# Loads of values and memory values get an earlier due time in the planner of a fused attention and MLP kernel

## The chip, the cores and the metric

The kernel runs on one core of a Trainium2 chip. The metric is the device time of one execution in microseconds, the median of several runs. Five engines run their own instruction streams in order: TensorE (PE, with its weight loads as PEld), VectorE (DVE), ScalarE (ACT), GpSimd (POOL) and SyncE (SP). SP computes nothing: it issues DMAs, one after the other, and an issue that waits for a semaphore holds back all that stand behind it.

## What is computed

```python
for c in range(nc):                       # 24 chunks of 32 rows, 4 batches, 8 heads of 64
    l_start = max(0, c * 32 - 16); r_end = min(S, c * 32 + 32 + 8)
    k_full = np.concatenate([mem_k, k[:, :, l_start:r_end]], axis=2)
    v_full = np.concatenate([mem_v, v[:, :, l_start:r_end]], axis=2)
    a = softmax(scale * q_c @ k_full^T)
    out[:, :, c_start:c_end] = a @ v_full
x = out.transpose(0, 2, 1, 3).reshape(3072, 512)
x = (sigmoid(x @ w_gate) * (x @ w_val)) @ w_out        # inner width 1536
h = x @ w_in                                           # inner width 2048
return (h * sigmoid(1.702 * h)) @ w_out2
```

All inputs are float32. Local attention with 8 memory rows gives 3072 rows of 512; two gated MLPs follow.

## The kernel before, in words

**Products.** The MLPs run as products of 128x128 weights and 512 columns, each operand split into a high and a low part, three products for one. `first_product` (L821, L828) multiplies the attention's rows with w_gate and w_val, the gating stands at L845 to L856, `gemm2` (L1020) multiplies with w_out. The second MLP is built from combined blocks (L1318, L1655) and takes the time from about 470 us on.

**Attention.** It is cut into 32 tiles of 96 rows (three chunks, 8 heads). Six prologue tiles run ahead of the first MLP product, with q and k transposed on TensorE (L436, L444) and with buffers of their own. The tiles after that run inside the first MLP. The last 23 of them are late tiles: their q and k are loaded in 32-row pieces (12 loads for q, 16 to 20 loads for the k of two tiles), transposed on DVE (L532 q, L540 k), the scores are computed on TensorE (L555), softmax runs on DVE and ACT (L572 to L615), POOL normalises (L623), DVE transposes the weights into `pt` (L670), and TensorE multiplies `pt` with the values (L704, "PV"). On TensorE the PV of one late tile and the scores of the next form one burst.

**Values.** `load_ctx` (L407) loads the values of a tile and its 8 memory values into `vn` (names `in_v_dram` and `in_mem_v_dram` in the profile): two loads, three for a tile at the edge of a batch, together 256 KB. All tiles but the prologue's share one buffer `vn`, so a tile's loads wait for the PV of the tile before. In the trace the buffers of q, k and the normalised weights bear the names of memory that they share: `f` is q of a late tile, `raw` is k or the normalised weights.

**What sets the order.** All instructions are tasks of one list scheduler (`Schedule`, L73 to L130). Going backwards, a task's due time is the smallest of its successors' due times less the latency between, less its own duration and less its `slack`. Going forwards, each engine takes of the tasks that are ready by the planner's clock the one with the lowest due time. A task's due time passes on to all that it depends on, so a lower due time of a load also lowers those of the PV whose buffer it takes over, and of what that PV needs. Bursts have due times on a fixed pace (L605). In the prologue the planner fills gaps that it expects on TensorE with dummy products (L885).

**Issue.** Only SP issues the loads of q, k and v. POOL issues its own DMAs: loads of weights of the second MLP (`p_raw`, L292, 512 KB) and stores of prepared weights (`wo_dram`, L1429 256 KB and L1432 512 KB).

Of the kernel before, what the change touches and what calls it, by code (L numbers as in the profile page):

```python
# [33 lines left out]
class Schedule:  # L34
# [9 lines left out]
    def add(self, eng, dur, fn, r=(), w=(), nbytes=0, due=None, slack=0.0, margin=0.0, hold=0.0):  # L44
        i = len(self.tasks)
        deps = set()
        for x in r:
            if x in self.writer:
                deps.add(self.writer[x])
        for x in w:  # L50
            if x in self.writer:
                deps.add(self.writer[x])
            deps.update(self.readers.get(x, ()))
        for x in r:
            self.readers.setdefault(x, set()).add(i)
        for x in w:
            self.writer[x] = i
            self.readers[x] = set()
        deps.discard(i)
        self.tasks.append(  # L60
            dict(eng=eng, dur=dur, fn=fn, deps=deps, nbytes=nbytes, due=due, slack=slack, margin=margin, hold=hold, succ=[])
        )
        return i
# [82 lines left out]
def kernel(  # L146
# [39 lines left out]
    add = sch.add  # L186
# [155 lines left out]
        add(*(("dve", 0.7) if low_dve else ("pool", c_pool(512))), low, r=[kf, ("w", slot, 0)], w=[("w", slot, 1)])  # L342


    def dma(dst, src, key, r=(), act=False, dur=0.45, pool=False):
        n = 8
        for d in src.shape:
            n *= d
        q_ = nc.gpsimd if pool else nc.scalar if act else nc.sync
        add("pool" if pool else "act" if act else "sp", dur, lambda: q_.dma_start(out=dst(), in_=src), r=list(r), w=[key], nbytes=n)  # L350

    class Bufs:

# [36 lines left out]
    def attention(t, bufs, banks, pe_path, extra=None, nth=0, last=False):  # L390
# [9 lines left out]
        T = bufs.t  # L400
# [4 lines left out]
        def load_ctx(name, src, mem, act=False):  # L405

            s0 = j * TQ - LEFT  # L407
            r0 = LEFT if j == 0 else 0
            r1 = TK - RIGHT if j == TPB - 1 else TK
            parts = [(r0, r1, src[b, :, s0 + r0 : s0 + r1, :]), (TK, P, mem[b])]  # L410
            if j == 0:
                parts.append((0, LEFT, src[b, :, 0:LEFT, :]))
            if j == TPB - 1:
                parts.append((r1, TK, src[b, :, S - RIGHT : S, :]))
            ks = []
            for i, (a, z, s) in enumerate(parts):
                ks.append((kk[name], i))
                dma(lambda a=a, z=z: T[name][a:z], s.rearrange("h s d -> s h d"), ks[-1], r=pre, act=act)
            for i in range(len(parts), 4):
                ks.append((kk[name], i))  # L420
            return ks

        pre = [bufs.gate] if bufs.gate else []
# [4 lines left out]
        if pe_path:  # L428
            ident = bufs.ident
            dma(lambda: T["qn"], q[b, :, j * TQ : (j + 1) * TQ, :].rearrange("h s d -> s h d"), kk["qn"], r=pre)  # L430
            kkn = load_ctx("kn", k, mem_k)
            load_ctx("vn", v, mem_v)

            def pe_q():
# [32 lines left out]
        else:  # L467
            koff, n, fresh = extra
            if n:
# [5 lines left out]
                for hp in range(2):  # L475
                    for x in range(2):
                        r = hp * D + x * CH
                        d = slice(x * CH, (x + 1) * CH)
                        for p in range(NP):
                            dma(  # L480
                                lambda r=r, p=p: T["kb"][r : r + CH, p, lo:hi, :],
                                k[b, 2 * p + hp, s0 + lo * CH : s0 + hi * CH, d].rearrange("(c r) d -> r c d", r=CH),
                                (kk["kb"], r, p),
                                r=pre,
                                dur=0.62,
                            )
                        kh = k[b].rearrange("(p two) s d -> two s p d", two=2)[hp]
                        if lo:
                            dma(
                                lambda r=r: T["kb"][r + LEFT : r + CH, :, 0, :],  # L490
                                kh[0 : CH - LEFT, :, d],
                                (kk["kb"], r, "edge"),
                                r=pre,
                            )
                        if hi < nb:
                            dma(
                                lambda r=r: T["kb"][r : r + CH - LEFT, :, nb - 1, :],
                                kh[S - CH + LEFT : S, :, d],
                                (kk["kb"], r, "edge"),
                                r=pre,  # L500
                            )
            kkb = [(kk["kb"], r, p) for r in range(0, P, CH) for p in (0, 1, 2, 3, "edge")]
            if fresh:
                for hp in range(2):
                    for x in range(2):
                        r = hp * D + x * CH
# [6 lines left out]
                    r=[(kk["mn"], r) for r in range(0, P, CH)],  # L513
                    w=[kk["mt"]],
                )
            kqb = []
            for hp in range(2):
                for x in range(2):
                    r = hp * D + x * CH
                    qh = q[b].rearrange("(p two) s d -> two s p d", two=2)[hp]  # L520
                    for c in range(NCK):
# [6 lines left out]
                            r=pre,  # L528
# [131 lines left out]
        else:  # L660
# [14 lines left out]
            def rest():  # L675
                load_ctx("vn", v, mem_v)
                tadd(
                    "pool",
                    0.95,
                    lambda: norm(nc.gpsimd, T["pn"][:, :, 0:CTX], (0, TQ), (0, CTX)),  # L680
                    r=ke + [kk["sm"]],
                    w=[(kk["pn"], 0)],
                )
                tadd("pool", 0.6, ev_norm, r=ke + [kk["sm"]], w=[(kk["pn"], 1)])
                for part in range(4):
                    tadd(
                        "dve",
                        0.88,
                        lambda part=part: ev_pt(part),
                        r=[(kk["pn"], 0), (kk["pn"], 1)],  # L690
                        w=[(kk["pt"], part)],
                    )
# [371 lines left out]
    for b in range(NB - 2):  # L1064
        n = BLK
# [834 lines left out]
```

## Time and profile before

| | |
|---|---|
| time, median of 3 runs | 1135.66 us (1134.58 to 1137.0) |
| the profiled execution's own time | 1138.62 us |
| its span, first to last instruction | 1136.8 us |
| mean granted TensorE clock | 0.995 |
| PE busy | 1122.9 us (99%) |
| DVE busy | 843.9 us (74%) |
| ACT busy | 588.6 us (52%) |
| POOL busy | 158.9 us (14%) |

The profile is of one execution; all durations are from it. Busy is the time in which an engine executes; issuing a DMA and waiting are not in it. The granted clock is the share of full speed that the chip allows TensorE in a stretch: 1.00 is 2.4 GHz and 0.50 is 1.2 GHz. A releaser is what an idle engine waited for last, inferred from semaphores; where the named one was long done, it was another of those waited for.

### The profile page before, as it was taken

The numbers are of one execution on the slowest core, as the hardware profiler recorded it, in microseconds if no ns is written. First come the engines' busy times: TensorE is split into PE (matmuls) and PEld (weight loads), VectorE is DVE, ScalarE is ACT, GpSimd is POOL, SyncE is SP. The second block draws the span as 40 slices with busy tenths as digits, with TensorE's granted clock in tenths as the row PEclk, the third lists the DMA queues.
The fourth block names the chain that finished last, engine by engine and source line by source line (L and its number), as shares of the span: only waits on it lengthen the run. The fifth ranks groups of instructions, "written<-read, shape, count | busy, mean of one in ns | idle before, by whom it ended". The sixth has DMA issues, their size and how long they took to land.

```text
span 1136.8 us, 19523 instructions
## 1 busy us (share of the span) xinstructions
PE 1122.9 (99%) x7190; PEld 939.3 (83%) x7190; DVE 843.9 (74%) x1440; ACT 588.6 (52%) x972; POOL 158.9 (14%) x209
## 2 busy tenths in 40 slices
PE   9999999999999989999999999999999999999998
PEld 7888899988888867788888888888888888888886
DVE  7999757776677769798887787969966359575366
ACT  6887622223222344576766678657445365354452
POOL 5332244122433112200001110000000000000000
PEclk9999999999999989999999999999999999999999
DMA  9666244334433555553545867777797676786526
GB/s 208 217 206 203 75 127 102 54 63 120 95 88 75 149 126 158 191 177 120 177 166 188 321 232 270 254 291 268 240 263 217 199 202 213 239 220 198 174 82 178
DMA packets 245903, 203.13 MB, mean 179 GB/s; under 512 B 170928, under 2 KB 191920, under 8 KB 245808
## 3 DMA queue, kind: packets, MB, share of 16 engines
q1 hardware_dynamic: 225696, 168.33, 51.2%
q0 software_dynamic: 6880, 24.12, 5.7%
q10 hardware_dynamic: 13232, 9.44, 2.6%
q8 instruction: 57, 0.93, 0.3%
q14 instruction: 38, 0.31, 0.1%
HBM read 151.49 MB, written 50.33 MB: 178 GB/s over the span
## 4 chain that ended last, share of the span: by engine, by line
PE 95%; DMA 2%; DVE 1%; SPq 1%; ACT 0%; issue 0%; DVEq 0%; ACTq 0%
PE bank L1318 30%; PE bank L1655 20%; PE bank L1020 17%; PE bank L821 15%; PE bank L828 8%; PE both L704 2%; PE both L555 2%; DMA f<-in_q_dram 1%; SPq L350 1%; PE bank L885 1%; PE bank L704 0%; PE bank L645 0%; DVE pt L670 0%; DMA qn<-in_q_dram 0%; PE bank L444 0%
## 5 line engine op out<-in xcount | busy, mean ns | idle before, releaser
L1318 PE MATMUL bank<-sb_x,sb_r 128*128 128x512 f32 x1512 | 347.1, 389 | 0.0
L1318 PEld LDWEIGHTS bank<-sb_x,sb_r 128*128 128x128 f32 x1512 | 283.8, 188 | 58.9
L1655 PE MATMUL bank<-wq,w 128*128 128x512 f32 x756 | 178.0, 389 | 0.0
L1655 PEld LDWEIGHTS bank<-wq,w 128*128 128x128 f32 x756 | 141.8, 188 | 29.9 <-issue 0.4
L821 PE MATMUL bank<-xh,w 128*128 128x512 f32 (+1 forms) x464 | 160.5, 357 | 0.0
L821 PE MATMUL bank<-xl,w 128*128 128x512 f32 (+1 forms) x464 | 159.4, 355 | 0.0
L1334 DVE TENSOR_TENSOR sb_s<-bank,sb_s 128x512 f32<-128x512 f32 x108 | 74.4, 690 | 83.1 <-PE bank L1318 75.2
L828 PE MATMUL bank<-xh,w 128*128 128x512 f32 (+1 forms) x464 | 110.4, 360 | 0.0
L821 PEld LDWEIGHTS bank<-xh,w 128*128 128x128 f32 x464 | 88.6, 191 | 13.0
L1020 PE MATMUL bank<-gh,wq 128*128 128x512 f32 (+1 forms) x448 | 98.8, 361 | 0.0
L821 PEld LDWEIGHTS bank<-xl,w 128*128 128x128 f32 x464 | 88.4, 190 | 12.2
L1330 ACT ACTIVATE sb_s<-bank 128x512 f32<-128x512 f32 x108 | 64.7, 600 | 52.2 <-PE bank L1318 51.5
L828 PEld LDWEIGHTS bank<-xh,w 128*128 128x128 f32 x464 | 79.0, 191 | 12.6 <-issue 0.2
L1020 PEld LDWEIGHTS bank<-gh,wq 128*128 128x128 f32 x448 | 76.5, 189 | 13.1
L670 DVE STREAM_TRANSPOSE pt<-raw 32x256 f32<-32x256 f32 x184 | 79.6, 433 | 4.4 <-POOL raw L623 1.1
L1626 DVE TENSOR_TENSOR wq<-xh_g,wq 128x1024 fp32r<-128x1024 f32 (+1 forms) x60 | 60.5, 1008 | 24.3 <-ACT wq L1623 23.9
L1623 ACT ACTIVATE wq<-xh_g 128x1024 fp32r<-128x1024 f32 (+1 forms) x60 | 53.3, 888 | 34.5 <-PE bank L1655 33.6
L853 ACT ACTIVATE gh<-sig 128x512 fp32r<-128x512 f32 (+1 forms) x58 | 32.4, 559 | 74.8 <-DVE sig L848 71.7
L845 ACT ACTIVATE sig<-bank 128x512 f32<-128x512 f32 (+1 forms) x58 | 30.5, 526 | 64.1 <-PE bank L828 63.1
L1655 PE MATMUL bank<-wq,w_e 128*128 128x512 f32 x252 | 62.5, 389 | 0.0
L623 POOL TENSOR_TENSOR raw<-e,sm 96x448 f32<-96x448 f32 (+2 forms) x69 | 38.9, 574 | 166.0 <-DVE sm L615 125.6
L848 DVE SCALAR_TENSOR_TENSOR sig<-sig,bank 128x512 f32<-128x512 f32 (+1 forms) x58 | 34.0, 586 | 30.1 <-PE bank L828 29.4
(215 smaller groups left out, 1666.3 us busy)
## 6 DMA issues: line engine op xcount, KB each, us to landing
sb_r<-wc_dram SPq DMA_DIRECT2D x133, 256.0 KB
w<-wo_dram SPq DMA_DIRECT2D x63, 512.0 KB
w_e<-wo_dram SPq DMA_DIRECT2D x21, 512.0 KB
wc_dram<-sb_r SPq DMA_DIRECT2D x15, 512.0 KB
wo_dram<-w POOLq DMA_DIRECT2D x14, 512.0 KB, 3.7
raw<-in_moe_w_out_dram SPq DMA_DIRECT2D x13, 512.0 KB
raw<-in_moe_w_in_dram SPq DMA_DIRECT2D x13, 512.0 KB
wf_dram<-f POOLq DMA_DIRECT2D x24, 256.0 KB, 2.6
```

Source lines behind the costliest of these rows:

```text
L623: eng.tensor_tensor(out=dst, in0=e3()[r, :, c], in1=T["sm"][r].to_broadcast([n, H, keys[1] - keys[0]]), op=ALU.mult)
L670: nc.vector.transpose(T["pt"][r * CH : (r + 1) * CH, :, c * CH : (c + 1) * CH], T["pn"][c * CH : (c + 1) * CH, :, kb * CH : (kb + 1) * CH],)
L821: nc.tensor.matmul(bank[bk][:, :n], w[:, 0, ts[t]], x[xb][:, t, c0 : c0 + n], start=t == 0 and x is xhs, stop=False)
L828: nc.tensor.matmul(bank[bk][:, :n], w[:, 1, ts[t]], xhs[xb][:, t, c0 : c0 + n], start=False, stop=t == NK - 1)
L848: nc.vector.scalar_tensor_tensor(out=sig[:, :n], in0=sig[:, :n], scalar=1.0, in1=bank[src_val][:, :n], op0=ALU.add, op1=ALU.mult)
L1020: nc.tensor.matmul(bank[into[m]][:, c0 : c0 + n], w[:, wi, m * P : (m + 1) * P], g[:, :n], start=f == 0 and j == 0 and c0 == 0, stop=f == ...
L1318: nc.tensor.matmul(bank[bk], w[:, o : o + P], xt[x, k][:, xl, :], start=first and k == 0 and wl == 0 and xl == 0, stop=k == 1 and wl == 1, ...
L1330: add("act", c_act(BLK), lambda: nc.scalar.activation(work[n], bank[bk], AF.Copy), r=[("bank", bk)], w=[n])
L1334: nc.vector.tensor_tensor(out=work[n], in0=bank[bk], in1=work[n], op=ALU.add)
L1623: nc.scalar.activation(quad[b_][:, c, 0, :], src(js), AF.Copy)
L1626: nc.vector.tensor_tensor(out=quad[b_][:, c, 1, :], in0=src(js), in1=quad[b_][:, c, 0, :].bitcast(F32), op=ALU.subtract)
L1655: nc.tensor.matmul(bank[bk], lhs, quad[b_][:, x, gl_, :], start=begin, stop=last and x == js[-1] and wl == 1, skip_group_check=not first,)
```

## The change

`dma()` gets an argument `slack` that it hands to `add`, and `load_ctx` passes 5.0 us of it for `vn`, and 0.0 for `kn`. The due time of each load of values and memory values is 5 us earlier in the planner, for late tiles and for prologue tiles. No instruction is added or removed but for dummy products.

```diff
-    def dma(dst, src, key, r=(), act=False, dur=0.45, pool=False):
+    def dma(dst, src, key, r=(), act=False, dur=0.45, pool=False, slack=0.0):
...
-        add("pool" if pool else "act" if act else "sp", dur, lambda: q_.dma_start(out=dst(), in_=src), r=list(r), w=[key], nbytes=n)
+        add("pool" if pool else "act" if act else "sp", dur, lambda: q_.dma_start(out=dst(), in_=src), r=list(r), w=[key], nbytes=n, slack=slack)
...
-                dma(lambda a=a, z=z: T[name][a:z], s.rearrange("h s d -> s h d"), ks[-1], r=pre, act=act)
+                dma(lambda a=a, z=z: T[name][a:z], s.rearrange("h s d -> s h d"), ks[-1], r=pre, act=act, slack=5.0 if name == "vn" else 0.0)
```

**Place A, SP, the late tile whose PV runs at 404 us.** `f_81` and `f_82` are q of two later tiles, `raw_78` and `raw_79` keys, `vn` the values. Before:

```order
L350 DMA vn<-in_v_dram 8x8x64
L350 DMA raw_79<-in_k_dram 32x7x32 x2
L350 DMA f_81<-in_q_dram 32x4x32 x12
L350 DMA f_82<-in_q_dram 32x4x32 x12
L350 DMA raw_78<-in_k_dram 32x7x32 x2
L350 DMA vn<-in_v_dram 104x8x64
L350 DMA vn<-in_v_dram 16x8x64
L350 DMA vn<-in_mem_v_dram 8x8x64
L350 DMA raw_78<-in_k_dram 32x7x32 x14
L350 DMA f_81<-in_q_dram 32x4x32
```

and now:

```order
L350 DMA vn<-in_v_dram 8x8x64
L350 DMA raw_79<-in_k_dram 32x7x32 x3
L350 DMA f_81<-in_q_dram 32x4x32 x12
L350 DMA f_82<-in_q_dram 32x4x32 x12
L350 DMA raw_78<-in_k_dram 32x7x32
L350 DMA vn<-in_v_dram 104x8x64
L350 DMA vn<-in_v_dram 16x8x64
L350 DMA vn<-in_mem_v_dram 8x8x64
L350 DMA raw_78<-in_k_dram 32x7x32 x15
L350 DMA vn<-in_v_dram 120x8x64
```

The 24 loads of q still stand ahead of this tile's values; of the two loads of keys behind them one has moved behind the values. Elsewhere in the late tiles the values move ahead by 0 to 4 loads (by 16 for the first of them), and the memory values now follow the values directly, where in several tiles up to 12 loads of q stood between.

**Place B, SP, prologue.** `kn_i`, `qn_i`, `vn_i` belong to prologue tile i, `vn_94` to tile 0. Before:

```order
L350 DMA kn_3_146<-in_k_dram 120x8x64
L350 DMA qn_3_145<-in_q_dram 96x8x64
L350 DMA kn_3_146<-in_mem_k_dram 8x8x64
L350 DMA vn_94<-in_v_dram 104x8x64
L350 DMA kn_4_157<-in_k_dram 120x8x64
L350 DMA vn_94<-in_v_dram 16x8x64
L350 DMA qn_4_156<-in_q_dram 96x8x64
L350 DMA vn_94<-in_mem_v_dram 8x8x64
L350 DMA kn_4_157<-in_mem_k_dram 8x8x64
L350 DMA vn_1_126<-in_v_dram 120x8x64
L350 DMA vn_1_126<-in_mem_v_dram 8x8x64
```

and now:

```order
L350 DMA vn_94<-in_v_dram 104x8x64
L350 DMA vn_94<-in_v_dram 16x8x64
L350 DMA vn_94<-in_mem_v_dram 8x8x64
L350 DMA kn_3_146<-in_k_dram 120x8x64
L350 DMA qn_3_145<-in_q_dram 96x8x64
L350 DMA kn_3_146<-in_mem_k_dram 8x8x64
L350 DMA vn_1_126<-in_v_dram 120x8x64
L350 DMA vn_1_126<-in_mem_v_dram 8x8x64
L350 DMA kn_4_157<-in_k_dram 120x8x64
L350 DMA qn_4_156<-in_q_dram 96x8x64
L350 DMA kn_4_157<-in_mem_k_dram 8x8x64
```

The values of tiles 0 and 1 now stand ahead of q and k of tiles 3 and 4, and in the same way those of tile 2 ahead of q and k of tile 5: one more set of 256 KB ahead of each of these three tiles.

**Place C, TensorE, the first PV that runs without scores (at 457 us before).** `w_754` and the like are weight slots, `gh` and `gl` the gated rows. Before:

```order
L821 MATMUL bank_68<-xh_721,w_755 128x512
L821 MATMUL bank_68<-xl_722,w_755 128x512
L704 MATMUL both<-pt,vn 64x96 x8
L828 MATMUL bank_68<-xh_721,w_755 128x512 x4
L821 MATMUL bank_69<-xh_721,w_756 128x512
```

and now:

```order
L1020 MATMUL bank_71<-gh_86,wq_744 128x512
L1020 MATMUL bank_72<-gh_86,wq_744 128x512
L1020 MATMUL bank_73<-gh_86,wq_744 128x512
L704 MATMUL both<-pt,vn 64x96 x8
L1020 MATMUL bank_70<-gl_88,wq_744 128x512
L1020 MATMUL bank_71<-gl_88,wq_744 128x512
```

The PV has moved from the middle of an L821/L828 group into a group of L1020. Counted in the order, 1940 products of 512 columns stood ahead of it and now 1928; the burst before it moved from product 1908 to 1904. So 32 products stood between the two, and now 24. The last PV moved from 1964 to 1968. The bursts up to product 1760 keep their places within 8 products, and then 1812 became 1800 and 1860 became 1844.

**Place D, POOL, at the same time.** `raw_80` are the normalised weights, `wo_dram` stores, `p_raw` loads of 512 KB. Before:

```order
L1432 DMA wo_dram<-w_108 128x2x512
L623 TENSOR_TENSOR raw_80<-e,sm 96x8x56
L623 TENSOR_TENSOR raw_80<-e,sm 64x8x8
L623 TENSOR_TENSOR raw_80<-e,sm 32x8x8
L1429 DMA wo_dram<-w_104 128x512
L1432 DMA wo_dram<-w_108 128x2x512
L292 DMA p_raw_4676<-in_moe_w_out_dram 128x512
L292 DMA p_raw_4675<-in_moe_w_out_dram 128x512
L623 TENSOR_TENSOR raw_80<-e,sm 96x8x56
L623 TENSOR_TENSOR raw_80<-e,sm 64x8x8
```

and now:

```order
L1432 DMA wo_dram<-w_108 128x2x512
L1432 DMA wo_dram<-w_104 128x2x512
L623 TENSOR_TENSOR raw_80<-e,sm 96x8x56
L623 TENSOR_TENSOR raw_80<-e,sm 64x8x8
L623 TENSOR_TENSOR raw_80<-e,sm 32x8x8
L1429 DMA wo_dram<-w_104 128x512
L1432 DMA wo_dram<-w_108 128x2x512
L292 DMA p_raw_4673<-in_moe_w_out_dram 128x512
L292 DMA p_raw_4672<-in_moe_w_out_dram 128x512
L1432 DMA wo_dram<-w_108 128x2x512
```

Two stores instead of one stand right ahead of the normalisation. Behind it come, as before, two stores and the two loads `p_raw`, and now a third store before the next normalisation.

## Rows read from the trace of the kernel before

**Rows 1.** Page, part 4: the chain that ended last, by engine.
```profile
PE 95%; DMA 2%; DVE 1%; SPq 1%; ACT 0%; issue 0%; DVEq 0%; ACTq 0%
```
**Rows 2.** Waits of TensorE, whole span: waiting line, releaser, total, times, longest.
```profile
PE both L704 <- DMA vn<-in_mem_v_dram: 4.1, 1, 4.1
PE both L704 <- DVE w L1422: 2.4, 1, 2.4
...
PE bank L436 <- DMA qn<-in_q_dram: 0.2, 1, 0.2
```
**Rows 3.** TensorE's timeline: start, us, line, out<-in, count, idle before and releaser.
```profile
389.38 0.80 PE L704 MATMUL both<-pt,vn 128*64 128x96 f32 x14
```
**Rows 4.** SP's timeline: start, us, line, out<-in, count of issues.
```profile
387.20 12.73 SPq L350 DMA_DIRECT2D f<-in_q_dram  x24
399.97 0.92 SPq L350 DMA_DIRECT2D raw<-in_k_dram  x2
400.99 0.91 SPq L350 DMA_DIRECT2D vn<-in_v_dram  x2
401.94 0.33 SPq L350 DMA_DIRECT2D vn<-in_mem_v_dram  x1
...
446.54 0.35 SPq L350 DMA_DIRECT2D vn<-in_v_dram  x1
```
**Rows 5.** Chain of waits, prologue and around both PVs: start, us, what.
```profile
26.89 1.14 PE bank L885 x10
...
401.94 2.30 DMA vn<-in_mem_v_dram
...
404.37 1.55 PE both L704 x16
405.92 1.02 PE both L555 x48
406.94 2.00 PE bank L828 x4
408.95 2.49 PE bank L821 x8
...
442.97 1.81 PE bank L821 x8
...
445.69 0.81 PE both L704 x16
446.50 0.68 PE both L555 x46
...
452.20 0.44 DVE pt L670
...
457.04 0.88 PE both L704 x16
457.92 1.88 PE bank L828 x4
459.79 2.66 PE bank L821 x8
```
**Rows 6.** Stretches: us, busy by engine, PEclk, DMA share, GB/s.
```profile
10.00:20.00 10.00, 8.90 (x244) 7.50 (x245) 7.43 (x19) 7.17 (x18) 5.81 (x7) 1.00 1.06 195
404.00:406.00 2.00, 1.63 (x28) 1.43 (x34) 0.00 (x0) 0.00 (x0) 0.00 (x0) 0.50 0.39 66
```
**Rows 7.** POOL's timeline, 442 to 458 us, DMA issues.
```profile
444.84 0.59 POOL L1429 DMA_DIRECT2D wo_dram<-w  x1
445.43 0.71 POOL L1432 DMA_DIRECT2D wo_dram<-w  x1
446.13 0.60 POOL L292 DMA_DIRECT2D p_raw<-in_moe_w_out_dram  x1
```
**Rows 8.** Packets of 447 to 450 us, and of 450 to 457: queue, packets, MB, share.
```profile
q0 software_dynamic: 153, 0.56, 78.7%
...
q1 hardware_dynamic: 1047, 0.26, 16.8%
```

## What the changed order will do: the prediction

> **What bounds the kernel now.** I read the chain that ended last first: PE holds 95% of it [rows 1], so the time moves only where PE stands idle, runs slowly, or is given other work. The change gives it none beyond a few dummy products, so the second view is what PE waited for. Over the span only two waits exceed 2 us, and both are PV (L704): 4.1 us put down to the memory values, and 2.4 us put down to DVE L1422 [rows 2].
>
> The first: the values' buffer was free at 389.38 + 0.80 = 390.2, when the PV before had read it [rows 3]. SP issued the next values only at 400.99, behind 24 loads of q that took it 12.73 us and two loads of keys of 0.92 us together [rows 4]. The memory values, issued at 401.94, landed 2.30 us later, and PV began at 404.37 [rows 5].
>
> The second is really one for the values too. The last of the transposes that it needs ended at 452.20 + 0.44 = 452.64 [rows 5], 4.4 us before PV began at 457.04 and about 2 us before PE was there (457.04 - 2.4 = 454.65). The values were issued at 446.54, at once when PV at 445.69 had freed the buffer [rows 4, 5], and 10.50 us passed from that issue to PV. At the first wait, 404.37 - 400.99 = 3.38 us were enough. What differs is POOL: two stores and a load, 256 + 512 + 512 KB, were issued at 444.84, 445.43 and 446.13 [rows 7]. From 447 to 450 only POOL's queue q0 had packets, and the values' 256-byte packets on q1 moved after 450 [rows 8].
>
> After each wait the granted clock falls to 0.50, the lower level of 1.2 GHz [rows 6]. What that costs is read from the chain: PV, scores, four products of L828 and eight of L821 took 1.55 + 1.02 + 2.00 + 2.49 = 7.06 us after the first wait. At full speed they take 0.81 + 0.68 + 4 x 0.227 + 1.81 = 4.21 us, with 1.81 / 8 = 0.227 us for a product [rows 5]. So 2.85 us are lost. After the second, 0.88 + 1.88 + 2.66 = 5.42 stand against 0.81 + 0.91 + 1.81 = 3.53, so 1.89 us. Both waits with their slow clock hold 4.1 + 2.85 + 2.4 + 1.89 = 11.2 us.
>
> **The change, part by part.** *The first wait.* The 24 loads of q stay ahead of the values (place A), since at that place SP meets them before the planner's clock has the buffer free. One load of keys moves behind: 0.92 / 2 = 0.46 us of SP's time [rows 4], so the values land 0.46 us earlier and PE waits 3.7 us in place of 4.1. Burst and PV stand at the same products. The slow clock stays as it is. Term: **-0.46**. The keys that are now behind belong to a later burst, over 12 us away.
>
> *The other late tiles.* There the values move by 0 to 4 loads of some 0.45 us, and PE doesn't wait for them now [rows 2]: nothing. The q and k loads that they pass come up to three issues later (1.3 us); they too are not waited for in that part.
>
> *The prologue.* Each of tiles 3, 4 and 5 gets its q and k behind one more set of values, 256 KB. From 10 to 20 us the DMA engines are full (share 1.06) at 195 GB/s [rows 6], so each set takes 1.34 us. PE was just waiting for a q here, 0.2 us [rows 2], so there is no reserve for at least one of these tiles. The delays don't add up, since the total to be loaded before the first product is the same: the upper bound is 1.34 us. Against it: the new order puts the eight transposes of tile 0's weights ahead of tile 4's q, work of about a PV's length, 0.81 us, by my estimate. Of the extra 1.34 us some 0.5 remain. Six dummy products fewer, at 1.14 / 10 = 0.114 us [rows 5], are 0.7 us less work, of which I count half. Term: **+0.2**, bounds -0.7 (all dummies gained) and +1.34.
>
> *The second wait.* Place C: 24 products, not 32, lie between the buffer's release and PV. PE is there 8 x 0.227 = 1.81 us earlier: before, 8.1 us after the values' issue (454.65 - 446.54), now 6.3 us after. Call X the time from the issue of the values to PV: PE waits X - 6.3, or nothing. All other products are done either before or after, so the end moves by the change of this wait alone, and of its slow clock. X was 10.50; the lower bound is the 3.38 of the first wait [rows 4, 5]. Which is nearer? The release of the buffer comes 4 products and 0.46 us earlier, 1.4 us in all, while POOL's third transfer, the load `p_raw` at 446.13, was issued only 0.4 us ahead of the values and waits for DVE, which is busy throughout. I take it that the values now pass this load, but not the two stores. The 10.50 - 3.38 = 7.1 us of delay I split by bytes: 512 of 1280 KB are 2.85 us. X becomes 7.65, the wait 1.35, and the slow clock costs the same 1.89. Term: 1.35 - 2.4 = **-1.0**. The bounds are -2.4 - 1.89 = -4.3 (X under 6.3) and +1.8 (X stays 10.5), or +2.8 if the wait, then 4.2 us, is followed by as long a slow stretch as the first (2.85 in place of 1.89). DVE's transposes had 2 us of cover before PE arrived; 1.81 of these are gone, and the new order wins back a little by keeping all eight transposes together. If they come last, PE waits some tenths.
>
> *Sum:* -0.46 + 0.2 - 1.0 = -1.3 us. Against the profiled execution's span of 1136.8 us that is 1135.5, and against its own time of 1138.62 it is 1137.3; that execution lies 2.96 us above the median. The sum is carried to the median: 1135.66 - 1.3 = **1134.4 us**. About 0.2% (2.27 us) is what a measurement of this kernel tells from no change: faster is below 1133.4, slower above 1137.9.
>
> **The rivals.** *The second wait goes away.* If the values pass the stores too, or POOL's transfers have drained by then, X is below 6.3. For it: 3.38 us at the other wait, and the earlier release. Against it: in the trace of before, values issued 0.4 us behind the last transfer waited for them all. Time: -0.46 + 0.2 - 4.3 = -4.6, 1131.1 us. The Trainium skill, page "DMA: Bandwidth & Descriptors", section "Queues, rings and completion order", says that each DMA engine goes round robin between queues packet by packet, by which the values would never stand behind POOL's bytes as a whole. By that rule this rival would be the likeliest; the rows of 447 to 450 us, with q0 alone [rows 8], don't agree with it here.
>
> *The second wait grows.* PV has been moved 8 products closer to the release while the load keeps its 10.50 us, because POOL's stores and loads move along with DVE and PE. Then PE waits 4.2 us and the clock stays low for as long as after the first wait: -0.46 + 0.2 + 1.8 + 0.95 = +2.5, 1138.2 us, slower. It decides from X of about 10.3 us on; with the slow clock no longer than before (+1.55, 1137.2) it counts as the same.
>
> *The change does what it says for all late tiles:* the values are loaded when the buffer is free, both waits go with their slow clock, -11.2 us, 1124.4 us. Against it: place A, where 24 loads of q still stand ahead; only if SP got through them much faster could this come.
>
> **How the numbers follow.** The forecast (the first wait shorter by one issue, the second in part) gets 0.42, of which 0.06 lie below 1133.4, where the slow clock is regained or X is near 6.3. The second wait gone: 0.28, all faster. Both gone: 0.04. The second wait grown: 0.26, of which 0.20 slower (with the prologue's upper bound added) and 0.06 the same. So faster 0.06 + 0.28 + 0.04 = 0.38, same 0.36 + 0.06 = 0.42, slower 0.20. The forecast's own range is 1133.0 to 1136.6: the prologue's bounds and half of the second wait's. The range for 8 in 10 reaches to both neighbours: 1130.9 (second wait gone) to 1138.6 (grown, with 0.4 us in the prologue).
>
> **What would show it.** In the profile after: the first wait at PV near 404 us, some 3.7 us, with SP's values again behind 24 loads of q. The second PV without scores: its wait between 0 and 4.2 us, and the time from the values' issue to it, X, tells which case it is. The first L821 should begin within -0.7 to +1.3 us of its place; a new PE wait for `qn` or `kn` there speaks for the prologue's upper bound. The forecast is wrong if a burst in between waits for DVE (L670, L540), for that is a cost that I put at nothing.

## The result: slower by half a per cent, and the profile after

| | before | after |
|---|---|---|
| time, median | 1136.22 us (1134.58 to 1137.0, 4 runs) | 1142.16 us (1140.95 to 1143.51, 4 runs) |
| ratio to before | | 1.0055, 95% interval 1.0037 to 1.0072 |
| profiled execution: time, span | 1138.62, 1136.8 us | 1140.95, 1138.8 us |

The change costs about 6 us. The two profiled executions differ by only 2.3 us, since that of before was slower than its median and that of after faster. Which wait belongs to the kernel and which to one execution is therefore the first question, and a second profile of each kernel (below) answers it.

TensorE's waits in the profile after (waiting line, releaser, total, times, longest), to be set beside [rows 2]:

```profile
PE both L704 <- DMA vn<-in_mem_v_dram: 6.9, 3, 3.8
PE bank L436 <- DMA qn<-in_q_dram: 1.4, 2, 1.0
...
PE both L555 <- DVE qt L532: 1.3, 2, 1.0
```

PV still waits for values, now at three places. New are two waits of the scores for `qt`, the queries that DVE transposes. PE's timeline of after names the places (start, us, line, out<-in, count, idle before and releaser):

```profile
273.00 0.71 PE L555 MATMUL both<-kt,qt 64*32 64x64 f32 x48 [0.97 <-DVE qt L532]
...
298.80 0.71 PE L555 MATMUL both<-kt,qt 64*32 64x64 f32 x48 [0.36 <-DVE qt L532]
...
405.21 1.55 PE L704 MATMUL both<-pt,vn 128*64 128x96 f32 x16 [3.77 <-DMA vn<-in_mem_v_dram]
...
433.08 0.88 PE L704 MATMUL both<-pt,vn 128*64 128x96 f32 x16 [2.85 <-DMA vn<-in_mem_v_dram]
```

The first long wait has shrunk from 4.14 to 3.77 us, the one at 457 to 0.24, and one of 2.85 us has appeared at 433, at a burst that waited for nothing before. The chain of waits through that place (start, us, what):

```profile
420.07 0.50 ACT qt L733
...
420.60 6.12 DMA x_dram<-qt
426.71 0.02 issue
426.73 0.31 SPq L350
...
430.15 2.79 DMA vn<-in_mem_v_dram
432.95 0.14 issue
433.08 0.88 PE both L704 x16
```

Read from the end: PV waited for the memory values, issued at 430.15. SP stood idle before 426.73, and what let it go on was the landing of a store, `x_dram`, which ScalarE had issued at 420.60 with the result of the late tile before. SP's timeline shows the stop as one long piece, nine loads of queries in 10.79 us:

```profile
418.30 0.43 SPq L292 DMA_DIRECT2D xl_y<-in_moe_w_in_dram  x1
418.83 10.79 SPq L350 DMA_DIRECT2D f<-in_q_dram  x9
429.72 0.39 SPq L350 DMA_DIRECT2D vn<-in_v_dram  x1
430.15 0.45 SPq L350 DMA_DIRECT2D vn<-in_mem_v_dram  x1
```

A load of queries has nothing to do with that store, but in these programs each issue from SP or ScalarE uses one of eight semaphores in turn, and waits until the issue that used it eight places before has landed. (In the trace the issues of both engines bear the numbers 101 to 105, 107, 108 and 110 over and over; the store has 107, and the load at 426.73 waits for 107.) In the program before, the store stands behind the eleventh of these twelve loads, and none of them comes back to its semaphore. In the changed program the burst that it belongs to stands at product 1800 instead of 1812, the store is issued among the loads of the tile ahead, and the fourth load of the next run has its semaphore. The store itself was slow: 6.12 us, where the same store took 2.9 to 3.0 us in both profiles of the kernel before. Shortly ahead of it GpSimd had issued two loads of 512 KB, right behind one another, and SP one more of 512 KB at 418.30. That these loads slowed it is likely, but no run shows it by itself (POOL's timeline):

```profile
418.86 1.12 POOL L292 DMA_DIRECT2D p_raw<-in_moe_w_out_dram  x2
```

So the values did move ahead of three loads of queries, as the change wants, and yet were issued at 429.72, where SP's timeline of before has 424.27, behind twelve loads without a stop:

```profile
417.17 6.99 SPq L350 DMA_DIRECT2D f<-in_q_dram  x12
424.27 0.46 SPq L350 DMA_DIRECT2D vn<-in_v_dram  x1
```

### The profile page after: what moved, and what is told of

The parts are those of the page before. It is cut to its first block, busy times and chain, and to the rows that moved or that the text cites. A ratio compares the mean times of both kernels' runs of the same rounds, so it can differ in the third digit from the quotient of the medians.

```text
span 1138.8 us, 19520 instructions
## 1 busy us (share of the span) xinstructions
PE 1120.1 (98%) x7184; PEld 935.8 (82%) x7184; DVE 839.5 (74%) x1440; ACT 588.6 (52%) x972; POOL 161.1 (14%) x209
## 4 chain that ended last, share of the span: by engine, by line
PE 86%; SPq 5%; DMA 4%; DVE 2%; ACT 1%; issue 1%; DVEq 0%; ACTq 0%
PE bank L1318 30%; PE bank L1655 20%; PE bank L1020 15%; PE bank L821 12%; PE bank L828 6%; SPq L350 5%; PE both L704 2%; PE both L555 1%; DMA x_dram<-qt 1%; DMA vn<-in_mem_v_dram 1%; DMA qn<-in_q_dram 0%; DMA y_dram<-f 0%; DMA w<-wo_dram 0%; DMA f<-in_q_dram 0%; DVE pt L670 0%
## 5 line engine op out<-in xcount | busy, mean ns | idle before, releaser
L821 PE MATMUL bank<-xh,w 128*128 128x512 f32 (+1 forms) x464 | 160.2, 356 | 0.3 <-ACT w L321 0.3
L821 PE MATMUL bank<-xl,w 128*128 128x512 f32 (+1 forms) x464 | 158.9, 353 | 0.0
L828 PE MATMUL bank<-xh,w 128*128 128x512 f32 (+1 forms) x464 | 110.5, 361 | 0.0
L821 PEld LDWEIGHTS bank<-xh,w 128*128 128x128 f32 x464 | 88.0, 190 | 13.7 <-ACT w L321 0.7
L1020 PE MATMUL bank<-gh,wq 128*128 128x512 f32 (+1 forms) x448 | 99.2, 362 | 0.0
L821 PEld LDWEIGHTS bank<-xl,w 128*128 128x128 f32 x464 | 88.0, 190 | 12.0
L828 PEld LDWEIGHTS bank<-xh,w 128*128 128x128 f32 x464 | 79.0, 191 | 12.6 <-issue 0.2
L1020 PEld LDWEIGHTS bank<-gh,wq 128*128 128x128 f32 x448 | 77.1, 191 | 13.2
L1655 PEld LDWEIGHTS bank<-wq,w_e 128*128 128x128 f32 x252 | 47.3, 188 | 9.8
```

Source lines behind the costliest of these rows:

```text
L821: nc.tensor.matmul(bank[bk][:, :n], w[:, 0, ts[t]], x[xb][:, t, c0 : c0 + n], start=t == 0 and x is xhs, stop=False)
L828: nc.tensor.matmul(bank[bk][:, :n], w[:, 1, ts[t]], xhs[xb][:, t, c0 : c0 + n], start=False, stop=t == NK - 1)
L1020: nc.tensor.matmul(bank[into[m]][:, c0 : c0 + n], w[:, wi, m * P : (m + 1) * P], g[:, :n], start=f == 0 and j == 0 and c0 == 0, stop=f == ...
L1655: nc.tensor.matmul(bank[bk], lhs, quad[b_][:, x, gl_, :], start=begin, stop=last and x == js[-1] and wl == 1, skip_group_check=not first,)
```

## The experiments

### Which part: the late tiles, or the prologue

```diff
-slack=5.0 if name == "vn" else 0.0
+slack=5.0 if name == "vn" and t >= NPRO else 0.0
```

> The earlier due time only for the tiles behind the prologue, the prologue's six tiles as in the kernel before. Theory P (the loss is made in the prologue, where values stand ahead of queries and keys): the time of the kernel before, 1136.2 us, within 1.5 us. Theory L (the loss is made by the late tiles, whose queries now land behind the values and make TensorE wait near 273 and 298 us, and by a second long wait for values near 433 us): 4 to 6 us above it, 1140 to 1142.

1141.57 us, ratio 1.0047 (1.0035 to 1.0059): nearly the whole loss. Waits of TensorE:

```profile
PE both L704 <- DMA vn<-in_mem_v_dram: 7.8, 2, 5.0
```

They stand at 405 (4.96 us) and at 433 (2.81 us). There is none for `qt` near 273 and 298, so those two are not what decides.

```diff
-slack=5.0 if name == "vn" else 0.0
+slack=5.0 if name == "vn" and t < NPRO else 0.0
```

> The earlier due time only for the six prologue tiles. Theory P: 1140 to 1142 us, TensorE waiting for a query near 13 us as in the changed kernel. Theory L: within 1.5 us of the kernel before (1136.2), although the prologue's waits are there, since the first real product starts at 34.6 us in the changed kernel and at 35.7 in the one before.

1138.44 us, ratio 1.0021 (1.0011 to 1.0030), between the two theories. The prologue is not free either, or it shifts the planner's clock so that the late tiles come out worse: its profile has a wait of 1.32 us at 298 and one of 1.33 us at 464 beside the 4.69 at 407, all in late tiles. The loss is mostly that of the late tiles (theory L).

### Which waits are always there: a second profile of each kernel

> The kernel before unchanged, for a second profile. If the two long waits of its first profile (4.1 us at 404 and 2.4 us at 457) are there in every execution, they stand in this profile too, within 1 us each. If they depend on how transfers happen to collide, at least one differs by more than 1.5 us: the first profile was 2.4 us above the median of the runs, so the typical execution should hold about 2.4 us less of them.

1135.57 us, ratio 0.9994 (0.9985 to 1.0004). The profiled execution took 1135.24 us. Its waits:

```profile
PE both L704 <- DMA vn<-in_mem_v_dram: 5.7, 3, 4.9
PE bank L885 <- POOL ident masks.py:199: 1.4, 1, 1.4
```

The first wait is there, with 4.88 us. The second, 2.4 us in [rows 2], is gone: the same program, with the same stores and loads of GpSimd around the values. So it is not there in every execution.

> The changed kernel unchanged, for a second profile. Its first profiled execution was at 1141.0 us, 1.2 below the median. If the loss lies in waits that are always there (0.97 and 0.36 us for late queries, 3.8 us near 405, 2.9 us near 433), they stand here again within 0.5 us each. If it lies in collisions, the wait near 433 is there with another size, or the one near 457 is back with 2 us or more.

1142.59 us, ratio 1.0061 (1.0047 to 1.0074).

```profile
PE both L704 <- DMA vn<-in_mem_v_dram: 7.1, 2, 3.7
...
PE both L555 <- DVE qt L532: 1.0, 2, 0.6
```

All of them again, within 0.6 us each: 3.69 us at 405, 3.43 at 432, 0.43 and 0.61 for `qt`. The chain shows the same store, with 6.95 us:

```profile
419.34 6.95 DMA x_dram<-qt
426.28 0.02 issue
426.30 0.31 SPq L350
```

And the clock falls behind the new wait as behind the old one (us, busy by engine, PEclk, DMA share, GB/s):

```profile
434.00:436.00 2.00, 2.00 (x22) 1.54 (x12) 1.60 (x3) 0.88 (x2) 0.00 (x0) 0.50 0.96 304
```

These two profiles, of executions 0.3 us (before) and 1.8 us (after) below their medians, can be laid beside each other by products done:

| PE at | before (e3) | after (e4) | lag |
|---|---|---|---|
| product 816 | 195.26 | 195.52 | +0.3 |
| burst at 1268 | 271.56 | 271.42 | -0.1 |
| burst at 1412 | 309.37 | 310.37 | +1.0 |
| burst at 1760 (PV of the first wait) | 405.74 | 404.95 | -0.8 |
| product 1964 | 461.93 | 465.93 | +4.0 |
| last product of the kernel | 1128.7 | 1133.8 | +5.1 |

(PE's timeline gives 466.84 for product 1968 in after; 4 x 0.227 are taken off for 1964.) Between 405 and 466 us 4.8 us are lost: 3.43 at 432, 0.37 at 457, and 1.0 in the slow clock. (Behind the wait at 432, PV, scores and sixteen products take 6.67 us where they take 5.1 at full speed, so some 1.6 us are lost; the slow stretch behind the first wait is about 0.6 us shorter than in the kernel before.) The prologue and the waits for `qt` together cost about 1 us. From there to the first wait 1.8 us come back: 1.2 of it is the shorter first wait, 0.5 a wait at 376 us that only this profile of before has. The last 1.1 us are lost behind 466 us and not explained, but for two waits of 0.30 and 0.16 us.

One thing of the second wait did come again. In the first profile of the changed kernel the values for that PV, 240 KB, were issued at 450.91, and from 451 to 453 us only GpSimd's queue q0 had packets (queue, packets, MB, share); the values' queue q1 moved 0.23 MB from 453 to 456, and PV waited 0.24 us:

```profile
q0 software_dynamic: 170, 0.63, 89.8%
```

### Is it the semaphore of the store?

```diff
-        q_ = nc.gpsimd if pool else nc.scalar if act else nc.sync
+        q_ = via if via is not None else nc.gpsimd if pool else nc.scalar if act else nc.sync
...
                         act=True,
+                        via=nc.gpsimd if t == 25 else None,
```

> The changed kernel, with one store changed: the x_dram store of the late tile whose PV runs at 418 us is issued by GpSimd instead of ScalarE, everything else in the same order. Theory R (the wait of 2.9 to 3.4 us at 433 us comes about because SP's fourth load of queries waits for the semaphore that this store used, 6.1 to 7.0 us after its issue, and the values stand five loads behind): SP's loads of queries run through, the values are issued before 426 us, the wait at 433 is gone with its slow clock, and the time falls by 3.5 to 5 us, to 1137 to 1138.7. Theory T (the transfers themselves are slow behind GpSimd's two loads of 512 KB, whoever waits for which semaphore): the values are still issued after 428 us and the time stays at 1142 within 1 us.

1137.71 us, ratio 1.0016 (1.0000 to 1.0032). Against the 1.0055 and 1.0061 of the changed kernel this single store, issued elsewhere, is worth 0.0039 to 0.0045, or 4.4 to 5.1 us, with some 2.5 us of uncertainty either way. SP's timeline (the profiled execution was the slowest of the ten, 4.2 us above the median, and ran some 5.5 us late before this place, with waits for `qt` of 1.17 and 2.06 us at 249 and 276):

```profile
424.08 4.28 SPq L350 DMA_DIRECT2D f<-in_q_dram  x9
430.73 0.33 SPq L350 DMA_DIRECT2D vn<-in_v_dram  x1
```

The nine loads take 4.28 us, as in a free queue, although the store still took 5.2 us to land. The values then wait only for their buffer, and PV doesn't wait at this burst. So it is the semaphore, not the transfers: theory R. The edit changes two things beside that: GpSimd's second load of 512 KB now stands behind the store, and every later issue of SP and ScalarE moves by one place in the turn of eight. What ties the stop to the semaphore is therefore this run together with the chain above, where SP's load goes on at the store's landing in both profiles.

### Do the values cost anything when they really go first?

A function behind the planner takes the finished order and moves, for a chosen tile, the loads of queries that stand directly ahead of its values (as far as nothing needs them before) right behind them:

```diff
+        order = values_first(order, {21: 24})
         assert len(order) == len(T)
```

> The kernel before, with one tile's values moved: in SP's order the values of the tile whose PV runs at 404 us stand ahead of 22 of the 24 loads of queries that stood ahead of them, the loads of queries right behind them. Theory Q (the wait of 4.1 to 4.9 us there is the length of the queue ahead of the values, with 2.85 us of slow clock behind it): the wait is gone, and the time falls by 6 to 8 us, to 1128 to 1130. Theory S (SP is busy without a break, so whoever is moved ahead only makes the next one late): the wait is gone, and queries or keys of the next burst make TensorE wait for 3 us or more, so that the time falls by less than 3 us.

1138.78 us, ratio 1.0021 (1.0005 to 1.0036): no gain, rather a small loss. The wait at 404 is gone; SP issues the values at 391.76, and 22 loads of queries after them (SP's timeline; the lines of this kernel are 29 higher, L733 is PV):

```profile
391.76 0.90 SPq L379 DMA_DIRECT2D vn<-in_v_dram  x2
392.71 0.76 SPq L379 DMA_DIRECT2D vn<-in_mem_v_dram  x1
393.51 12.21 SPq L379 DMA_DIRECT2D f<-in_q_dram  x22
405.77 6.81 SPq L379 DMA_DIRECT2D raw<-in_k_dram  x14
412.68 0.39 SPq L379 DMA_DIRECT2D f<-in_q_dram  x1
413.16 0.38 SPq L379 DMA_DIRECT2D vn<-in_v_dram  x1
```

But the next tile's values come at 413.16 (410.58 before), and now its PV waits:

```profile
418.57 1.54 PE L733 MATMUL both<-pt,vn 128*64 128x96 f32 x16 [3.62 <-DMA vn<-in_mem_v_dram]
434.10 0.88 PE L733 MATMUL both<-pt,vn 128*64 128x96 f32 x16 [1.41 <-issue]
```

The queue ahead of that tile has taken over the wait: theory S, though not quite as expected, since it is again values that come late, not queries or keys.

```diff
+        order = values_first(order, {21: 24, 23: 9})
```

> The changed kernel, with the values of two tiles moved as its title says, ahead of the queries: at 404 us ahead of 23 loads of queries, at 433 us ahead of 9. Theory R and Q together: both waits are gone, the time falls by 10 to 12 us against the changed kernel, to 1130 to 1132. Theory S: less than 5 us.

1139.34 us, ratio 1.0021 (1.0002 to 1.0040). By the ratios some 4 of the 6 to 7 us come back. In the profile the wait at 433 is gone, but the one at 404 has gone to 418 with 4.8 us, and one of 2.5 us has appeared at 458. The profiled execution was the slowest of ten, 4.4 us above the median, so the size of these two is not that of a typical one; the time alone (less than 5 us regained) says S again.

```diff
+        order = values_first(order, None)
```

> The kernel before, with the values of every late tile moved ahead of all queries that are not needed before them (10 to 22 loads for most tiles). Theory Q: as e6, 1128 to 1130 us, since the other tiles did not wait for values before. Theory S: the loads of queries that are now behind the values come up to 2 us later for nearly every tile, new waits for DVE's transposed queries appear as at 272 and 298 us in the changed kernel, and the time is 2 us or more above e6.

1158.84 us, ratio 1.0197 (1.0171 to 1.0223): by far the worst. This is the order that the change aims at, taken to its end for every late tile; the other engines keep the order that was planned without it. TensorE's waits, and one of DVE's that the kernel before does not have:

```profile
PE bank L850 <- DVE sig L877: 9.0, 2, 6.3
PE both L584 <- DVE qt L561: 8.2, 4, 3.7
PE both L733 <- DMA vn<-in_mem_v_dram: 3.2, 1, 3.2
...
DVE qt L561 <- DMA f<-in_q_dram: 25.3, 9, 4.9
```

The scores wait for late queries (L561 is their transposition), and DVE, which stands behind these in its own order, comes late with the gating (L877) for everybody.

### Take the values out of SP's queue

If SP's time is what is short, the values need another issuer. ScalarE waits for every late burst in any case, to evict it (L733 or L758 of the kernel before), so by then the buffer is free.

```diff
-                load_ctx("vn", v, mem_v)
+                load_ctx("vn", v, mem_v, act=True)
```

> The kernel before, with the values and memory values of the late tiles issued by ScalarE instead of SP, two or three issues a tile. Theory S (SP has no time left between 142 and 425 us: some 24 issues of 0.45 to 0.5 us a tile against 12 to 13 us of products, so that a load moved ahead makes another late): with the values out of SP's queue both they and the queries are in time, the wait of 4.1 to 4.9 us at 404 and its slow clock are gone and nothing takes their place: 7 us less than the kernel before, about 1129 us. Theory C (the wait is one of transfers that are slow behind GpSimd's loads): the values still land late and the time stays within 2 us.

1128.26 us, ratio 0.9931 (0.9916 to 0.9945), faster than both kernels. No PV waits any more; the longest waits left are

```profile
PE bank L885 <- POOL ident masks.py:199: 1.4, 1, 1.4
PE bank L436 <- DMA qn<-in_q_dram: 0.8, 2, 0.7
```

both in the prologue. SP's timeline now has longer pauses; here it issues nothing from 395.82 to 399.88:

```profile
385.42 7.18 SPq L350 DMA_DIRECT2D f<-in_q_dram  x12
392.65 3.17 SPq L350 DMA_DIRECT2D raw<-in_k_dram  x6
399.88 10.09 SPq L350 DMA_DIRECT2D f<-in_q_dram  x15
```

Counted in the trace, SP issues 190 DMAs between 300 and 400 us in the kernel before, at about 0.5 us each with the step between them, and 168 in this one. Its pauses of 0.3 us and more add up to 4.7 us there and to 14.5 us here. The queue is full only up to about 425 us: behind that the kernel before has pauses of 4 to 10 us. So the first wait comes where the queue is nearly full (in the two profiles of the kernel before, pauses of 1.7 and 3.2 us stand shortly ahead of the 24 loads), while the one at 433 comes from the stop.

> The changed kernel with the same edit: the values of the late tiles issued by ScalarE. Theory S: the waits at 272, 298, 405 and 433 us all go, and the earlier due time has nothing left to spoil: within 1.5 us of the kernel before with the same edit, about 1129 us. If the earlier due time costs by itself, through the places of the bursts, it stays 3 us or more above that.

1129.48 us, ratio 0.9938 (0.9924 to 0.9952): the earlier due time does no measurable harm once the values are out of SP's queue (0.9938 beside 0.9931, with intervals that overlap over most of their length). In both runs the stores, too, have other semaphores than before, so the two causes, SP's time and the stop at the store, are not separated here.

> The earlier due time for the six prologue tiles alone, with the late tiles' values issued by ScalarE, so that SP's queue no longer turns a shift of the plan into a wait for values. If the prologue's own price is near nothing, as its place in the products says (at product 816 the changed kernel stands within 0.3 us of the second profile of the kernel before), the time is that of the kernel before with the values on ScalarE, 1128.3 us, within 1 us. If the values ahead of queries and keys in the prologue cost the 2.4 us of the run with the prologue alone, it is 1130.5 us or more.

The edits of the second and the ninth kernel together: 1130.07 us, ratio 0.9950 (0.9936 to 0.9964). By the ratios that is 2.2 us above the kernel without the earlier due time, and with both intervals anything from about 0 to 4 us. In the profile the prologue's own part is small: the first late place on PE, a PV, comes at 43.51 instead of 43.04 us, and a wait of 0.6 us near 172 follows. The prologue's price is not settled better than "0.5 us seen, some 2 us possible".

## Why the prediction was wrong, point by point

- **The first wait** (term -0.46). Right in kind: one load of keys less ahead of the values, 24 loads of queries still there, and the wait shorter by 0.4 us in the first profiles (4.14 and 3.77) and by 1.2 in the second ones (4.88 and 3.69). With the late tiles alone changed both loads of keys stand ahead again, and the wait was 4.96 us. One kernel's own wait differs by 0.7 us between two executions, so the size of the term is neither confirmed nor refuted.
- **The other late tiles** (term nothing). **This is the step that failed.** The prediction counted what the loads moved in SP's order, 0 to 4 issues of 0.45 us, and found that nothing waited there. It didn't ask what the issues wait for, nor how full the queue was. An earlier due time of the values also brought bursts forward (place C: 1812 to 1800, 1860 to 1844). With a burst moves its store, and with the store a semaphore that SP's queue comes back to. That cost 2.85 us at 433 in the first profile and 3.43 us at 432 in the second, each with some 1.6 us of slow clock behind it; taking that one store out of the turn brought 4.4 to 5.1 us back. The part of the prediction that lists what would prove it wrong named a burst that waits for DVE; these waits came too, for late queries (`qt`, L532), and cost about 1 us, but the large one was a wait for values.
- **The second wait** (term -1.0, one rival at -4.3, another at +2.8). Right reading, wrong use: in that execution PV did wait for values that were slow behind GpSimd's transfers, but the second profile of the same kernel has no such wait, and there was nothing to gain in it. In the changed kernel PE stood ready 6.29 us after the issue of the values in both profiles, as worked out (6.3). X was 6.5 and 6.7 us, not 7.65, and the wait 0.24 and 0.37 us, not 1.35. The reason given for 7.65 did not hold: both loads `p_raw` were issued ahead of the values there (448.98 and 450.12 against 450.91), and the one at 446.13 had waited for nothing before. The profiled execution stood 2.96 us above the median, and the prediction said so; it should have asked which of its waits was the surplus.
- **The prologue** (term +0.2). Its direct price is not refuted: at product 816 after is 0.3 us behind in the second profiles and 0.4 ahead in the first. With all that follows in the late tiles, the kernel with the prologue alone was 2.4 us slower (1.2 to 3.4), more than the upper bound of 1.34; how much of that is the prologue's own is open (last experiment).
- **The rival "the second wait grows"** came nearest in time (1138.2), and that by luck: the mechanism was another, at another burst. There too the burst came earlier in the order while the load got less time than it needs: here the load's issue itself came 5.45 us later (429.72 and 424.27).
- **The rival "does what it says for all late tiles"** was priced at -11.2 us. The nearest experiment (e8) says about +22: the wait that goes comes back on queries, because up to 425 us SP has no time to give.
- **The rule of the Trainium skill** on round robin between queues ("DMA: Bandwidth & Descriptors", "Queues, rings and completion order") was set against the rows of 447 to 450 us. The long wait stood in one of two executions, but q0 alone was seen in the changed kernel too (451 to 453 us, above). So the rows go on disagreeing with the rule as the prediction used it. Whether the values' packets were ready in the queue by then, no view shows; the reason stays open.

## What to carry to other kernels

Before moving a DMA ahead in a queue, count how full the queue is: SP here issued 190 DMAs in 100 us at 0.5 us each, so in all three trials the loads that went first made others late, and only taking issues out of the queue (to ScalarE, which was waiting for the same event anyway) gained time, 0.7%. List for every issue what it waits for, reused semaphores and stores of other engines included, since a queue that runs in order passes one slow transfer on to everything behind it. And price a wait only when more than one execution shows it, above all when the profiled run lies off the median.

## What the runs showed of the hardware that was not expected

- A store of 192 KB that landed 6.12 and 6.95 us after its issue stopped the queue of another engine for 6.5 and 4.8 us. Issued by GpSimd, with 5.2 us to land, it stopped nothing.
- The same program shows a wait of 2.4 us in one execution and none in another, with the transfers around it issued at the same distances to within about 1 us.
- An engine without arithmetic decided about 8 us of the 1136: with some issues taken off SyncE the time fell by that much, while TensorE was busy throughout from 200 to 400 us and the DMA engines had a share of 0.41 (kernel before).
